# The last scatters, the gates' store, the rows' sum and the last output's scaling in a fused attention and expert kernel: what changes in their order

## The chip, the cores and the metric

The kernel runs on one core of one Trainium2 chip. The metric is the device time of one execution in microseconds (us). TensorE (PE in the profile, its weight loads PEld), VectorE (DVE), ScalarE (ACT), GpSimd (POOL) and SyncE (SP) each run their own instructions in order, and wait for each other by semaphores.

## The reference

Windowed attention over 8 batches, 8 heads, 576 positions and head size 64 gives 4608 rows of 512. Each row then goes to the one expert of eight that its gate logits choose:

```python
x = attn_out.transpose(0, 2, 1, 3).reshape(B * S, H * D)      # 4608 x 512
logits = x @ w_gate                                           # 4608 x 8
expert_idx = argmax(logits, axis=1)
gate_w = softmax(logits)[row, expert_idx]
for e in range(8):
    xe = x[expert_idx == e]
    out[expert_idx == e] = gate_w * (relu(xe @ w1[e]) @ w2[e])   # 512 -> 1024 -> 512
```

All of it is fp32; each large product is made from high and low parts (fp32r).

## The kernel before

**Attention.** The four pairs of batches are cut into nine tiles of 128 rows, 36 steps in all. A step works on several tiles at once, in different stages, and the rows that come out are stored by POOL to `x_d` in DRAM. The first 35 steps stand in a hand-written order; the last ones and the rest up to the experts are ordered by the framework, which keeps the order of the code for each engine except where its model of times puts an instruction earlier. Each row of `x_d` has 512 values of x and 16 copies of the row's gate behind them.

**Routing.** After each pair `route(m)` turns its logits into places: the maximum (`mx`, `sh`), the first expert that has it (`cand`, `fst`, `oh`), counts (`cs`), exponentials and the gate (`ex`, L437 by a helper; `se`, `gate`), which L614 copies sixteen times into `many` and L615 stores by POOL into the last 16 columns of the pair's 1152 rows of `x_d`, 64 bytes a row. Three matmuls with the running counts `crun` give each row's rank in its expert (`rk`, L522 to L526); L530 (`sel`) picks it, and L625 to L632 make from it a position: its block (`blk_i`) and its place in it (`plc_i`).

The positions are written down in two ways. For the first three pairs, each tile of 128 rows is entered by a scatter (L542): an indirect DMA that POOL issues, and that writes row numbers to one of three tables `tab` in DRAM, at the addresses `at_i` that `place` computes. The nine scatters of a pair are put in a list, `slow`, from which every attention step takes one (`pull_spaced`), so the third pair's are issued during the last steps. For the last pair, a table is built in PSUM: `mark` (L557 to L568) makes for each tile a one-hot `s` (by ACT over `off`, or by DVE at L560) and a one-hot `b`, and `enter` (L579) multiplies them into `tb`, in three groups of three. Its steps stand in another list, `side`, in which `off_pe` and `off_both` put work of the other engines and `on_pe` that of TensorE; `pull_pe` and `pull_off` take from it.

**From the tables to the rows.** When all scatters are done, SP reads the three tables into `t_in` (L675) and POOL adds them (L680, L681); DVE makes `scr` from `tb` (L662, L666) and adds the two into `rows_all` (L437 by the helper), which lists the row of every slot of every expert. POOL then gathers rows: `xg<-x_d` (L752), 128 rows and their gates at a time, and these feed the blocks of the experts over transposes by TensorE (`tpx`, L976 and L852).

**Experts.** Meanwhile TensorE works on rows already known, those of expert 0's first tile. Weights come in units of 512 KB (`raw`, L885), which ACT and DVE split into high and low parts (`wu`, L726 and L727). Layer one gives `hps` (L906), from which ACT and DVE make `h` (L917, L918); layer two gives `yps` (L937). After the eight experts and the extra blocks, a loop runs `left` times more, a count that each engine loads from `left` (L1649); in this run it is nought. `finish` (L801) scales `yps` by the gate into `y` on ACT and scatters it to the output by POOL (L802).

Of the kernel before, what the change touches and what calls it, by code (L numbers as in the profile page):

```python
# [11 lines left out]
I32 = mybir.dt.int32  # L12
BF16 = mybir.dt.bfloat16
AF = mybir.ActivationFunctionType
ALU = mybir.AluOpType
# [45 lines left out]
NTHR = 40  # L61
NWARM = 9
GAP, FREE = 3, 35

C_ID, C_TRI, C_REV, C_C0, C_NEW, C_IO, C_ATT = np.cumsum(
    [0, P, P, NE, NE, NE * NT, P]
# [96 lines left out]
def attention_moe_kernel(ctx, tc, qk, v, wg, w, cst, tok, end, slots, mask, zero, out):  # L163
# [30 lines left out]
    sp = att.enter_context(tc.tile_pool(name="sp", bufs=4))  # L194

    late = att.enter_context(tc.tile_pool(name="late", bufs=1))
    t_in = [late.tile([P, NBK], I32, name=f"t_in{i}") for i in range(3)]

    NRQ, NRV = 6, 6
    qkr = fix.tile([P, NRQ, QK], F32, name="qkr")  # L200
# [226 lines left out]
            )  # L427
            lo = end

    side, slow, spare = [], [], []  # L430
    taken = [False]

    def on_pe(f, *a, late=False):
# [28 lines left out]
            side.pop(0)[1]()  # L462

    def pull_spaced():
        if slow:
            slow.pop(0)()

    def pull_off():
# [5 lines left out]
    def route(m, then=None, after=None):  # L474
# [54 lines left out]
        def select():  # L529
            v.tensor_tensor(sel, box["rk"], oh, op=ALU.mult)  # L530
            taken[0] = False

        def place(t):

            t = slice(t, t + 1)
            v.scalar_tensor_tensor(
                at_i[:, t], blk_i[:, t], -(NBK - 1.0 / P), wide[:, t], op0=ALU.mult, op1=ALU.add
            )

        def scatter(t, to, what):  # L540
            place(t)
            nc.gpsimd.indirect_dma_start(  # L542
                out=to[t % 3][:],
                out_offset=bass.IndirectOffsetOnAxis(ap=at_i[:, t : t + 1], axis=0),
                in_=what,
                in_offset=None,
            )
# [25 lines left out]
        def enter(ts):  # L573
# [3 lines left out]
            for t in ts:  # L577
                s1, b1 = hot.pop(t)
                nc.tensor.matmul(box["tb"], lhsT=s1, rhs=b1, start=t == 0, stop=t == NT - 1)  # L579

        on_pe(turn, (0, 1), late=True)
        off_pe(gather_parts, 0)
        off_pe(gather_parts, 1)
# [6 lines left out]
        off_both(  # L590
            lambda: v.scalar_tensor_tensor(cand, sh, 0.0, rev, op0=ALU.is_ge, op1=ALU.mult),
            lambda: v.tensor_reduce(fst, cand, axis=AX.X, op=ALU.max),
        )
        off_both(
            lambda: v.tensor_tensor(
# [8 lines left out]
                op1=ALU.add,  # L604
            ),
        )
        off_pe(nc.scalar.activation, ex, sh, AF.Exp)
        off_both(
            lambda: v.tensor_reduce(se, ex, axis=AX.X, op=ALU.add),
            lambda: v.tensor_scalar_add(se2, se, 1e-9),  # L610
# [1 line left out]
                gate, se2  # L612
            ),
            lambda: v.tensor_copy(many, gate.broadcast_to([P, NT, XP - DM])),  # L614
            lambda: nc.gpsimd.dma_start(  # L615
                x_d[DUMMY + m * S2 : DUMMY + (m + 1) * S2, DM:].rearrange("(t p) o -> p t o", p=P),
                many,
            ),
        )
        if m == NPR - 2:  # L620
            off_pe(hold, True)
# [12 lines left out]
        if m < NPR - 1:  # L634
            off_both(
                lambda: v.tensor_tensor(load, rows_i[:, m], plc_i, op=ALU.subtract),
                lambda: v.tensor_copy(load[:, ::3], rows_i[:, m, ::3]),
                lambda: v.tensor_scalar_mul(wide, posf, float(NBK)),
            )

            def enter_pair():
                v.tensor_tensor(crun, crun, cs[:, :, NT - 1], op=ALU.add)
                for t in range(NT):
                    spaced(scatter, t, tabs, load[:, t : t + 1])
                if then:
                    spaced(then)

            off_pe(enter_pair)
        else:
            off_both(  # L650
                lambda: v.tensor_copy(blk, blk_i),
                lambda: v.tensor_copy(plc, plc_i),
                lambda: v.tensor_tensor(pay, rows_f, plc, op=ALU.subtract),
            )
            off_pe(lambda: v.tensor_tensor(crun, crun, cs[:, :, NT - 1], op=ALU.add))
            for lo in range(0, NT + 3, 3):
                for t in range(lo, min(lo + 3, NT)):
                    off_pe(mark, t)
                if lo:
                    on_pe(enter, range(lo - 3, lo), late=True)  # L660
            off_pe(
                lambda: v.tensor_scalar(  # L662
                    scr, box["tb"], 0.0, float(LAST), op0=ALU.is_gt, op1=ALU.mult
                )
            )
            off_pe(lambda: v.tensor_tensor(scr, box["tb"], scr, op=ALU.add))  # L666
            off_pe(v.tensor_tensor, row_i, t_in[0], scr, op=ALU.add)
        if after:
            after()

# [125 lines left out]
        nc.scalar.copy(x[:, 0], rows)  # L796
        nc.vector.tensor_tensor(x[:, 1], rows, x[:, 0].bitcast(F32), op=ALU.subtract)  # L797

    def finish(y_ps, gate, it_col):
        y = pools["y"].tile([P, DM], F32, name="y")  # L800
        nc.scalar.activation(y, y_ps, AF.Copy, scale=gate)  # L801
        nc.gpsimd.indirect_dma_start(  # L802
            out=out,
            out_offset=bass.IndirectOffsetOnAxis(ap=it_col, axis=0),
# [4 lines left out]
    class Static:  # L809
# [115 lines left out]
                )  # L925
                self.h.append(h)

        def layer2(self, i, fs_=range(8)):
            if fs_[0] == 0:
                self.yps[i] = pools["ps"].tile([P, DM], F32, tag="C", name="yps")  # L930
            yps = self.yps[i]
# [10 lines left out]
                        stop=f == 7 and k == 2,  # L942
                    )
            if fs_[-1] == 7:
                finish(yps, self.gate[i], self.it[i])

    class Dynamic:
        def __init__(self, ti=None, wi=None, fixed=None, units=None, turned=False):
# [300 lines left out]
        step(n)  # L1249
        n += 1  # L1250
    assert not todo and not spare and not turning
    while slow:
        slow.pop(0)()
    while side:
        side.pop(0)[1]()
# [182 lines left out]
    for f in range(4, 8):  # L1438
        st_.layer1([f])
        raw = early.pop(f) if f in early else st_.load(f)  # L1440
        st_.units.append(split_unit(1, raw))
    r0, r1 = rest0
    with tc.manual_schedule(engines=ENGS | {mybir.EngineType.Pool, mybir.EngineType.SP}):
        ahead = nx.ahead
# [100 lines left out]
    with tc.manual_schedule(engines=ENGS | {mybir.EngineType.Pool, mybir.EngineType.SP}):  # L1545
# [97 lines left out]
        dy.layer2()  # L1643
        dz.layer2()
        st_.layer2(2)
        st_.layer2(3)

    left, nbig = info["left"], info["big"]
    extra = nc.values_load(left[0:1, 0:1], min_val=0, max_val=NTHR)  # L1649
    dcur = dsp.tile([P, 1], F32, name="dcur")  # L1650
    nc.vector.memset(dcur, float(DBIG))
    dnum = dsp.tile([P, 1], F32, name="dnum")
# [44 lines left out]
```

## Time and profile before

| | us |
|---|---|
| median of 3 runs | 605.0 |
| the three runs | 604.55, 605.0, 606.33 |
| profiled execution | 608.32 |
| its span | 606.5 |
| PE busy in the span | 587.6 (97%) |
| DVE, ACT, POOL busy | 361.7, 319.0, 185.6 |
| mean granted clock | 0.985 |

A row of the profile gives the line, the engine, the operation and `out<-in` by the names of the program. In rows in order of time the two first numbers are the start and the duration, `x` and a number is how many instructions the row holds, and the bracket is the idle time of the engine ahead of it, with what ended it. In grouped rows the numbers behind the bar are the busy time of all, the mean of one in ns, and idle times. A row with an engine's name and a q is its sequencer.

### The profile page before, as it was taken

What the parts mean: (1) busy time and instruction counts of PE and PEld (TensorE: products, weight loads), DVE (VectorE), ACT (ScalarE), POOL (GpSimd) and SP (SyncE); (2) the same over time, 40 slices, a digit from 0 to 9 for tenths busy, and PEclk for the clock granted to TensorE, in tenths of its full rate; (3) what the DMA queues carried; (4) which work ended last, traced back from release to release, by engine and by line L of the source; (5) the groups of instructions that cost most, each with busy time, mean ns of one, the idle gap of its engine ahead of it and who ended that gap; (6) DMA issues with size and microseconds to landing.
All of it is one profiled execution on the core that took longest, in us unless ns stands there. A gap on an engine that the chain in (4) does not pass through costs nothing. (4 is left out here: it accounts for less than half of the span.)

```text
span 606.5 us, 13511 instructions
## 1 busy us (share of the span) xinstructions
PE 587.6 (97%) x5175; PEld 480.4 (79%) x5175; DVE 361.7 (60%) x780; ACT 319.0 (53%) x624; POOL 185.6 (31%) x234
## 2 busy tenths in 40 slices
PE   7999999999899999999999999999999999999995
PEld 6877777777777888888888888888888887788784
DVE  3876887977668457636564666466555655663200
ACT  2568766666744555534555465455645553562210
POOL 0246577376484225130022012202401220021011
PEclk7899999999899999999999999999999999999998
DMA  8999999995216538986679688788877886789411
GB/s 323 409 367 413 412 407 405 394 340 152 85 52 212 175 124 272 241 289 181 190 261 333 144 266 273 243 222 269 285 232 202 258 294 172 225 267 403 178 44 45
DMA packets 67522, 152.52 MB, mean 251 GB/s; under 512 B 15040, under 2 KB 31360, under 8 KB 67424
## 3 DMA queue, kind: packets, MB, share of 16 engines
q1 hardware_dynamic: 55744, 121.50, 59.4%
q0 software_dynamic: 11712, 30.14, 14.5%
q8 instruction: 41, 0.67, 0.5%
q14 instruction: 25, 0.20, 0.1%
HBM read 124.02 MB, written 28.60 MB: 252 GB/s over the span
## 5 line engine op out<-in xcount | busy, mean ns | idle before, releaser
L727 DVE TENSOR_TENSOR wu<-raw,wu 128x512 fp32r<-128x512 f32 x200 | 128.7, 689 | 61.8 <-ACT wu L726 53.8
L937 PE MATMUL yps<-wu,h 128*128 128x512 f32 x696 | 164.4, 392 | 0.0
L906 PE MATMUL hps<-x,wu 128*128 128x512 f32 (+1 forms) x720 | 161.3, 383 | 0.4 <-DVE h L918 0.4
L906 PEld LDWEIGHTS hps<-x,wu 128*128 128x128 f32 x720 | 132.3, 188 | 27.2 <-DVE h L918 0.8
L937 PEld LDWEIGHTS yps<-wu,h 128*128 128x128 f32 x696 | 129.5, 188 | 27.4 <-issue 0.6
L726 ACT CAST wu<-raw 128x512 fp32r<-128x512 f32 x200 | 112.5, 618 | 11.5 <-DMA raw<-in_w_dram 11.2
L802 POOL DMA_INDIRECT out_dram<-y,rows_all x30 | 30.4, 1014 | 196.1 <-ACT y L801 109.1
L918 DVE SCALAR_TENSOR_TENSOR h<-hps,h 128x512 fp32r<-128x512 f32 (+1 forms) x60 | 40.2, 671 | 52.9 <-ACT h L917 50.2
L323 ACT COPY pts<-pt 96x512 f32<-96x512 f32 x72 | 41.9, 582 | 49.8 <-PE pt L318 40.9
L917 ACT ACTIVATE h<-hps 128x512 fp32r<-128x512 f32 (+1 forms) x60 | 35.0, 583 | 54.5 <-PE hps L906 52.8
L752 POOL DMA_INDIRECT xg<-x_d,rows_all x30 | 30.8, 1027 | 95.9 <-DVE x L797 45.2
L297 DVE TENSOR_REDUCE nm<-s 128x4 f32<-128x384 f32 x72 | 39.6, 551 | 28.1 <-PE s L286 21.3
L318 PE MATMUL pt<-ident,p 128*96 128x128 f32 x288 | 48.2, 292 | 5.2 <-ACT pts L323 4.1
L801 ACT ACTIVATE y<-yps,gate 128x512 f32<-128x512 f32 x30 | 20.6, 688 | 48.9 <-PE yps L937 39.0
L333 PEld LDWEIGHTS o<-vr,pts 96*64 96x64 f32 x1152 | 38.6, 140 | 7.5 <-issue 6.3
L333 PE MATMUL o<-vr,pts 96*64 96x65 f32 x1152 | 44.0, 227 | 0.5 <-issue 0.4
L302 DVE TENSOR_TENSOR d<-s,nm 128x384 f32<-128x384 f32 x72 | 40.0, 557 | 4.6
L1043 PE MATMUL ypd<-wu,hd 128*128 128x512 f32 x168 | 41.0, 392 | 0.2
L312 ACT ACTIVATE p<-d 128x384 f32<-128x384 f32 x72 | 37.6, 524 | 5.7 <-DVE d L302 5.7
L365 POOL DMA_DIRECT2D x_d<-xs x36 | 20.6, 571 | 64.6 <-DVE xs L353 28.4
L318 PEld LDWEIGHTS pt<-ident,p 128*96 128x96 f32 x288 | 29.3, 130 | 13.6 <-ACT pts L323 5.2
L1011 PE MATMUL hpd<-wu,xd 128*128 128x512 f32 x168 | 39.9, 391 | 0.0
(163 smaller groups left out, 626.8 us busy)
## 6 DMA issues: line engine op xcount, KB each, us to landing
raw<-in_w_dram SPq DMA_DIRECT2D x104, 512.0 KB
qkr<-in_qk_dram SPq DMA_DIRECT2D x36, 576.0 KB
vr<-in_v_dram SPq DMA_DIRECT2D x36, 520.0 KB
rows<-xg SPq DMA_DIRECT2D x29, 264.0 KB
xg<-rows SPq DMA_DIRECT2D x116, 64.0 KB
wu<-in_w_dram SPq DMA_DIRECT2D x12, 512.0 KB
x_d<-xs POOLq DMA_DIRECT2D x44, 128.0 KB
wz<-in_w_dram SPq DMA_DIRECT2D x4, 512.0 KB
```

Source lines behind the costliest of these rows:

```text
L297: nc.vector.tensor_reduce(st["nm", n][:, g], st["s", n][g], axis=AX.X, op=ALU.max)
L302: nc.vector.tensor_tensor(st["d", n][:, g], st["s", n][g], st["nm", n][:, g].broadcast_to([P, HP, KB]), op=ALU.subtract,)
L318: nc.tensor.transpose(pt[:KB, h], st["p", n][:, g, h], ident)
L323: nc.scalar.copy(st["pts", n][:, g], st.pop(("pt", n))[:KB])
L333: nc.tensor.matmul(st["o", n][QB * j : QB * (j + 1), g, h], lhsT=pts[:, g, h, QB * j : QB * (j + 1)], rhs=vr[:KB, n % NRV, a : a + DH + 1] ...
L726: nc.scalar.copy(u[:, 0, sl], raw[:, sl])
L727: nc.vector.tensor_tensor(u[:, 1, sl], raw[:, sl], u[:, 0, sl].bitcast(F32), op=ALU.subtract)
L906: nc.tensor.matmul(hps[:, : self.ns], lhsT=u[:, wpart, fs], rhs=self.x[:, xpart, c, : self.ns], start=(k == 0), stop=(k == 11),)
L918: nc.vector.scalar_tensor_tensor(h[:, 1, :n], hps[:, :n], 0.0, h[:, 0, :n].bitcast(F32), op0=ALU.max, op1=ALU.subtract,)
L937: nc.tensor.matmul(yps, lhsT=self.h[f][:, hpart, ts], rhs=u[:, wpart, fs], start=f == 0 and k == 0, stop=f == 7 and k == 2,)
L1011: nc.tensor.matmul(hps, lhsT=self.x[:, xpart, c], rhs=u[:, wpart, ns], start=(k == 0), stop=(k == 11),)
L1043: nc.tensor.matmul(self.yps, lhsT=self.h[f // 4][:, hpart, f % 4], rhs=u[:, wpart, fs], start=f == 0 and k == 0, stop=f == 7 and k == 2,)
```

## The change

The diff, cut to its core (the `t_in` tiles also move: the first one from the pool `late` to the pool `const`):

```diff
+KEPT = 4
...
     def pull_spaced():
-        if slow:
+        if slow and (now[0] < total or len(slow) > KEPT):
             slow.pop(0)()
...
         def select():
             v.tensor_tensor(sel, box["rk"], oh, op=ALU.mult)
             taken[0] = False
-
-        def place(t):
-
-            t = slice(t, t + 1)
-            v.scalar_tensor_tensor(
+            if m == NPR - 1:
+                while slow:
+                    slow.pop(0)()
+                tc.keep_in_program_order(keep_gates())
+
+        def place(lo, hi):
+
+            t = slice(lo, hi)
+            return v.scalar_tensor_tensor(
                 at_i[:, t], blk_i[:, t], -(NBK - 1.0 / P), wide[:, t], op0=ALU.mult, op1=ALU.add
             )

         def scatter(t, to, what):
-            place(t)
+            if now[0] < total or t < NT + 1 - KEPT:
+                place(t, t + 1)
+            elif t == NT + 1 - KEPT:
+                tc.keep_in_program_order(place(t, NT))
             nc.gpsimd.indirect_dma_start(
...
+        def keep_gates():
+            return nc.gpsimd.dma_start(
+                x_d[DUMMY + m * S2 : DUMMY + (m + 1) * S2, DM:].rearrange("(t p) o -> p t o", p=P),
+                many,
+            )
+
...
             lambda: v.tensor_reduce(fst, cand, axis=AX.X, op=ALU.max),
+            lambda: nc.scalar.activation(ex, sh, AF.Exp),
         )
...
-        off_pe(nc.scalar.activation, ex, sh, AF.Exp)
...
-            lambda: nc.gpsimd.dma_start(
-                x_d[DUMMY + m * S2 : DUMMY + (m + 1) * S2, DM:].rearrange("(t p) o -> p t o", p=P),
-                many,
-            ),
+            lambda: None if m == NPR - 1 else keep_gates(),
...
-            off_pe(v.tensor_tensor, row_i, t_in[0], scr, op=ALU.add)
+            finals.append(lambda: v.tensor_tensor(row_i, t_in[0], scr, op=ALU.add))
...
-    def finish(y_ps, gate, it_col):
+    def finish(y_ps, gate, it_col, halved=False):
         y = pools["y"].tile([P, DM], F32, name="y")
-        nc.scalar.activation(y, y_ps, AF.Copy, scale=gate)
+        own = DM // 2 if halved else DM
+        nc.scalar.activation(y[:, :own], y_ps[:, :own], AF.Copy, scale=gate)
+        if halved:
+            nc.vector.tensor_scalar_mul(y[:, own:], y_ps[:, own:], gate)
...
-    while slow:
+    while len(slow) > KEPT:
         slow.pop(0)()
...
         raw = early.pop(f) if f in early else st_.load(f)
         st_.units.append(split_unit(1, raw))
+        if f == 5:
+            tc.keep_in_program_order(finals.pop()())
...
         st_.layer2(2)
-        st_.layer2(3)
-
-    left, nbig = info["left"], info["big"]
-    extra = nc.values_load(left[0:1, 0:1], min_val=0, max_val=NTHR)
+        left, nbig = info["left"], info["big"]
+        extra = nc.values_load(left[0:1, 0:1], min_val=0, max_val=NTHR)
+        st_.layer2(3, halved=True)
+
```

The list `slow` of the third pair ends with the step that reads the tables. `KEPT = 4` keeps that step and the three scatters ahead of it (tiles 6 to 8) from being taken once attention's 36 steps are over; `select` of the last pair takes them, right behind `sel`. `keep_in_program_order` holds an instruction in its place against the framework's reordering.

On POOL, at the end of the routing, before: `tab_64` to `tab_66` are the three tables, `t_in_108` to `t_in_110` their copies.

```order
L542 DMA tab_65<-load,at_i 40960x1
L542 DMA tab_64<-load,at_i 40960x1
L542 DMA tab_66<-load,at_i 40960x1
L615 DMA x_d<-many 128x9x16
L680 TENSOR_TENSOR t_in_108<-t_in_108,t_in_109 128x320
L681 TENSOR_TENSOR t_in_108<-t_in_108,t_in_110 128x320
L752 DMA xg<-x_d,rows_all 128x528 x5
```

And the same place after the change, where the scatter is L550, the store L590, the adds L691 and L692 and the gather L763, with what each waits for in brackets (the semaphores of POOL's DMA queues are DMASW, those of SP's DMAHW):

```order
L550 DMA tab_64<-load,at_i 40960x1 [waits DMASW7_49,DVE_49]
L550 DMA tab_65<-load,at_i 40960x1 [waits DMASW6_49]
L550 DMA tab_66<-load,at_i 40960x1 [waits DMASW0_49]
L691 TENSOR_TENSOR t_in_108<-t_in_108,t_in_109 128x320 [waits DMAHW7_49,DMAHW0_49]
L692 TENSOR_TENSOR t_in_108<-t_in_108,t_in_110 128x320 [waits DMAHW1_49,Pool_49]
L590 DMA x_d<-many 128x9x16 [waits DMASW4_49]
L763 DMA xg<-x_d,rows_all 128x528 [waits DMASW5_49,DMASW4_49,DVE_49]
```

The gates' store has moved from ahead of the two adds to behind them, and the gather waits, as before, for the store's landing (DMASW4) and for `rows_all` on DVE; the first of the three scatters now waits for DVE's merged `at_i`.

On DVE, from the last group's `h` to the next ones, before and after; the `wu` are split weights, `scr` the last pair's rows:

```order
L918 SCALAR_TENSOR_TENSOR h<-hps,h 128x256
L662 TENSOR_SCALAR scr<-tb 128x320
L727 TENSOR_TENSOR wu<-raw,wu 128x512
L666 TENSOR_TENSOR scr<-tb,scr 128x320
L727 TENSOR_TENSOR wu<-raw,wu 128x512
L437 TENSOR_TENSOR rows_all<-t_in_108,scr 128x320
L918 SCALAR_TENSOR_TENSOR h<-hps,h 128x256
L727 TENSOR_TENSOR wu<-raw,wu 128x512 x2
```

```order
L932 SCALAR_TENSOR_TENSOR h<-hps,h 128x256
L673 TENSOR_SCALAR scr<-tb 128x320
L738 TENSOR_TENSOR wu<-raw,wu 128x512
L677 TENSOR_TENSOR scr<-tb,scr 128x320
L738 TENSOR_TENSOR wu<-raw,wu 128x512
L932 SCALAR_TENSOR_TENSOR h<-hps,h 128x256
L738 TENSOR_TENSOR wu<-raw,wu 128x512 x2
L678 TENSOR_TENSOR rows_all<-t_in_108,scr 128x320
```

`rows_all` has moved behind one `h` and two `wu`. Also on DVE, one `at_i` over 128x3 stands between `many` and `posf`, where before the nine single ones had all come earlier.

At the end of the program, after the change, ACT's last rows, DVE's last and POOL's last scatter, each with its waits:

```order
L813 ACTIVATE y<-yps,gate 128x512 [waits DMASW2_49,DMASW4_49,DVE_49,PE_49]
L813 ACTIVATE y<-yps,gate 128x256 [waits DMASW3_49,DMASW5_49,DVE_49,PE_49]
L815 TENSOR_SCALAR y<-yps,gate 128x256 [waits DMASW5_49,Activation_49]
L816 DMA out_dram<-y,rows_all 4736x512 [waits DMASW6_49,DVE_49]
```

Before, the last of these `y` was one ACTIVATE of 128x512 that waited for PE, and the scatter waited for ACT. Now the DVE half waits for ACT's half, and the scatter for DVE. The load of `left` by each engine moved from behind the last `layer2` to ahead of it; SP's moved from the middle of the program to the end with it.

More of the change, by code (lines that the diff above doesn't have):

```diff
@@ L196, in attention_moe_kernel @@
     late = att.enter_context(tc.tile_pool(name="late", bufs=1))
-    t_in = [late.tile([P, NBK], I32, name=f"t_in{i}") for i in range(3)]
+    t_in = [(const, late, late)[i].tile([P, NBK], I32, name=f"t_in{i}") for i in range(3)]
     NRQ, NRV = 6, 6
@@ L428, in st_keep @@
             lo = end
-    side, slow, spare = [], [], []
+    side, slow, spare, finals = [], [], [], []
     taken = [False]
@@ L926, in layer1, with layer2 @@
                 self.h.append(h)
-        def layer2(self, i, fs_=range(8)):
+        def layer2(self, i, fs_=range(8), halved=False):
             if fs_[0] == 0:
@@ L944, in layer2 @@
             if fs_[-1] == 7:
-                finish(yps, self.gate[i], self.it[i])
+                finish(yps, self.gate[i], self.it[i], halved)
     class Dynamic:
```

## The prediction

> **What bounds the kernel now.** I read the page first, then the stretches, then the order of time around the last selection, then the DMA queues there and the end. The page says that TensorE is nearly always busy. The stretches (length, then busy time of PE, PEld, DVE, ACT and POOL) say where it is not.
>
> ```profile
> PE 587.6 (97%) x5175; PEld 480.4 (79%) x5175; DVE 361.7 (60%) x780; ACT 319.0 (53%) x624; POOL 185.6 (31%) x234
> ...
> 170.00:215.00 45.00, 42.88 (x251) 35.76 (x251) 27.88 (x76) 22.67 (x55) 19.97 (x21) 1.00 0.44 141
> 215.00:500.00 285.00, 285.00 (x1280) 236.03 (x1279) 169.21 (x288) 150.98 (x273) 64.03 (x62) 1.00 0.78 243
> 500.00:580.00 80.00, 79.47 (x400) 63.01 (x399) 37.68 (x64) 33.06 (x61) 6.86 (x8) 1.00 0.70 238
> ```
>
> From 215 to 500 us PE has no idle time, from 500 to 580 it has 0.53 us. So time taken out of PE's waits before 215 comes off the end in full, and time put in is never made up. What there is to take is 45.00 - 42.88 = 2.12 us between 170 and 215, where the change works; the one other place that it touches is the end. Now the last selection in order of time (start, duration, idle time and its releaser), with the same step of the previous pair ahead of it:
>
> ```profile
> 166.07 0.39 PE L526 MATMUL rk<-cs,cc 128*128 128x72 f32 x2
> ...
> 166.50 0.23 DVE L530 TENSOR_TENSOR sel<-rk,oh 128x72 f32<-128x72 f32 x1 [0.27 <-PE rk L526]
> ...
> 177.33 0.44 PE L526 MATMUL rk<-cs,cc 128*128 128x72 f32 x2
> 177.48 0.96 POOL L542 DMA_INDIRECT tab<-load,at_i  x1 [0.30 <-issue]
> ...
> 178.54 0.23 DVE L530 TENSOR_TENSOR sel<-rk,oh 128x72 f32<-128x72 f32 x1 [0.84 <-PE rk L526]
> ...
> 178.75 0.97 POOL L542 DMA_INDIRECT tab<-load,at_i  x1 [0.30 <-issue]
> ...
> 179.21 0.17 DVE L630 CAST pos<-posf 128x9 int32<-128x9 f32 x1
> ...
> 180.01 0.69 ACT L557 ACTIVATE off<-ca,plc 128x128 f32<-128x128 f32 x2 [3.04 <-DVE plc L652]
> 180.02 0.97 POOL L542 DMA_INDIRECT tab<-load,at_i  x1 [0.30 <-DVE plc L652]
> ...
> 180.99 1.06 POOL L615 DMA_DIRECT2D x_d<-many  x1
> 181.04 0.41 PE L579 MATMUL tb<-b,s 128*128 128x320 f32 x1 [1.00 <-ACT off L557]
> ...
> 181.32 0.77 DVE L560 TENSOR_SCALAR s<-ca,plc,pay 128x128 fp32r<-128x128 f32 x1
> ...
> 182.15 0.42 PE L579 MATMUL tb<-b,s 128*128 128x320 f32 x1 [0.32 <-DVE s L560]
> ...
> 182.77 0.34 DVE L560 TENSOR_SCALAR s<-ca,plc,pay 128x128 fp32r<-128x128 f32 x1
> ```
>
> In the previous pair `sel` starts 0.04 us after the rank matmuls end (166.46 to 166.50). Here they end at 177.77 and `sel` starts at 178.54, 0.77 later, 0.10 after a scatter on POOL ends (178.44). From `sel` a chain runs over `pos`, `plc` and ACT's `off` to the first `tb` matmul, for which PE idles 1.00 us. The third group waits for DVE's `s`, which took 0.77 us beside the gates' store on POOL (180.99 to 182.05), against 0.34 at 182.77: 0.43 lost, 0.32 of it on PE.
>
> **The three scatters behind the selection.** The scatters at 177.48, 178.75 and 180.02 go behind `sel`. If `sel` was late because POOL was at them, it comes 0.73 sooner (0.77 - 0.04). Ahead of `posf` now stands one `at_i` over 128x3; the nearest row is `pos`, 0.17. The three single ones that go had lain earlier, beside attention, and free nothing. So the chain to `off` gains 0.73 - 0.17 = 0.56 at the first `tb`. With the store away, `s` gains up to 0.32 more on PE: 0.88. From below: the three scatters now run beside the chain, from about 178.5 to 182.2, and if they delay PE's signals as before, half of it is left, 0.4. From above it is both idles whole, 1.00 + 0.32 = 1.3. I take 0.7, nearer to the worked sum than to the ends. Merged `at_i`, exponentials and the first read of the three tables cost nothing beyond this: on DVE and ACT the exponentials keep their place, and SP only reads the tables in another order.
>
> **The gates' store and the rows.** What follows is the second wait that the change touches; the adds, the rows, the gathers and the first use of what they bring:
>
> ```profile
> 184.04 0.39 ACT L917 ACTIVATE h<-hps 128x256 fp32r<-128x256 f32 x1 [0.42 <-DVE s L560]
> ...
> 184.46 0.42 DVE L918 SCALAR_TENSOR_TENSOR h<-hps,h 128x256 fp32r<-128x256 f32 x1 [0.50 <-ACT h L917]
> ...
> 184.82 0.88 POOL L680 TENSOR_TENSOR t_in<-t_in,t_in 128x320 int32<-128x320 int32 x1 [2.77 <-DMA t_in<-tab]
> ...
> 185.78 1.21 POOL L681 TENSOR_TENSOR t_in<-t_in,t_in 128x320 int32<-128x320 int32 x1
> ...
> 187.46 0.48 DVE L437 TENSOR_TENSOR rows_all<-t_in,scr 128x320 int32<-128x320 int32 x1
> ...
> 188.20 1.35 DVE L727 TENSOR_TENSOR wu<-raw,wu 128x512 fp32r<-128x512 f32 x2
> 188.22 1.02 POOL L752 DMA_INDIRECT xg<-x_d,rows_all  x1 [1.23 <-DVE rows_all L437]
> ...
> 189.00 1.47 PE L937 MATMUL yps<-wu,x 128*128 128x512 f32 x5 [0.44 <-DVE wu L727]
> ...
> 195.91 0.59 PEld L976 LDWEIGHTS tpx<-ident,xg 128*128 128x128 f32 x4
> ...
> 200.71 0.60 PE L852 MATMUL tpx<-ident,xg 128*128 128x128 f32 x4
> ```
>
> `rows_all` moves behind an `h` (0.42) and two `wu` (1.35). That lets those pass: PE's 0.44 at 189.00 can go, but only if DVE isn't the next thing late, so I leave it as the upper end and count nothing. By itself `rows_all` then starts about 187.46 + 1.77 - 0.7 = 188.5.
>
> The gathers also wait for the gates' store, since it writes part of the rows that they read. Before, it started at 180.99 and was long done at 188.22. Now it stands behind the adds. The last scatter starts at about 181.1 in place of 180.02, and with it the read of the last table; without the store beside them the reads may run a little quicker, so I put the end of the adds where it was, at 186.99, and let it go as far as 188. Then the store's 1.06 us, and its landing. How long that takes, and a gather's landing, is read from POOL's queue (q0: packets, MB, share of the DMA engines), in the stretch 184 to 185.6 (from 185.6 to 187 there are no packets at all), then 190 to 191 with the weights' queue q1 ahead of it, 191 to 192, and 192 to 193:
>
> ```profile
> q0 software_dynamic: 12, 0.01, 1.7%
> ...
> DMA packets 0, 0.00 MB, mean 0 GB/s; under 512 B 0, under 2 KB 0, under 8 KB 0
> ...
> q1 hardware_dynamic: 157, 0.38, 96.0%
> q0 software_dynamic: 1, 0.00, 1.0%
> ...
> q0 software_dynamic: 64, 0.24, 65.4%
> ...
> q0 software_dynamic: 16, 0.04, 33.8%
> ```
>
> The store's last packets move after 184 and before 185.6, so it lands 3.0 to 4.6 us after its start. The gather of 188.22 has nothing moved by 191 and its 0.28 MB done by 193: 3.8 to 4.8 us, beside weights that fill the DMA engines. Now: store at 187.0, landed at 190.0 to 191.6, first gather then, 2 to 3 us later than before, landed 3.8 to 4.8 after that, 193.8 to 196.4. PE wants it at 195.91 less the gain, 195.2. So the cost lies between 0 and 1.2 us; with the adds as late as 188 it is up to 2.2. I take 0.4, below the middle of 0 to 1.2, since most of the earliest-to-latest stretch lies before the need. The next gather's rows are wanted at 200.71, five microseconds later, and gathers follow each other by 1.3, so they add nothing.
>
> The Trainium skill ("DMA: Bandwidth & Descriptors", section "Anatomy of one DMA — SWDGE (gpsimd) path") gives a DMA issued by GpSimd about 2.0 us plus its bytes at 436 GB/s. By that page the 72 KB store would land after an estimated 2.2 us, at 189.2, and the cost here would be 0; the trace does not agree, with at least 3.0, and the sum keeps the trace's.
>
> **The end.** PE's last matmuls, the last output's scaling, its scatter; then the weight of such an output by form, and of one without a factor from SBUF; then where `left` is loaded, for each engine's sequencer:
>
> ```profile
> 594.74 5.15 PE L937 MATMUL yps<-wu,h 128*128 128x512 f32 x22
> ...
> 599.92 0.69 ACT L801 ACTIVATE y<-yps,gate 128x512 f32<-128x512 f32 x1 [4.75 <-PE yps L937]
> 600.90 0.97 POOL L802 DMA_INDIRECT out_dram<-y,rows_all x1 [2.51 <-ACTq L1653]
> ...
> L801 ACT ACTIVATE y<-yps,gate 128x512 f32<-128x512 f32 x30 | 20.6, 688 | 48.9 <-PE yps L937 39.0 <-issue 7.4 <-ACT wu L726 2.4
> ...
> L1019 ACT ACTIVATE hs<-hpd 128x512 f32<-128x512 f32 x14 | 8.4, 598 | 19.8 <-PE hpd L1011 18.4 <-issue 1.3
> ...
> L1649 PEldq TENSOR_LOAD <-left x1: 545/545/545, 595.7 to 595.7; - x1
> ```
>
> The last `y` becomes ACT on 256 columns and DVE on 256. In the changed order DVE's half waits for ACT's, not for PE, so they run one behind the other. ACT's half costs 0.39 (the `h` of 128x256) plus the 0.09 by which a scaled 512 (0.688) exceeds a plain one (0.598): 0.48. A hand-off is 0.03 (184.43 to 184.46) and DVE's half is like the `h` of 0.42. Sum 0.93 against 0.69: 0.24 slower, and nothing hides it, as POOL's scatter waits for `y`. Side by side it would be 0.69 - 0.48 = 0.21 quicker. I take +0.25, since the wait is in the order.
>
> The Trainium skill ("PSUM — Partial Sum Buffer", section "PSUM bank collisions raise a hardware error") says that no two engines may touch the same PSUM bank and partitions at once, readers too, and that the compiler orders them. It speaks against this halving: by it the sum is +0.24, without it -0.21. No run here shows two engines in one bank at once.
>
> `left` is now loaded ahead of the last 24 matmuls. PE's sequencer ran its load (0.545) at 595.7, over four microseconds ahead of the last matmul's end at 599.89. That lead hides it; were it gone, it would cost 0.55.
>
> **The sum.** -0.7 (selection) + 0.4 (gather) + 0.25 (end) = -0.05, so nothing. The profiled execution took 608.3 us, 606.5 of it span; it would be 608.3 again, and it lies 3.3 over the median of 605.0, which both keep. I forecast 605.0.
>
> **The rivals.**
> *Full gain.* Both idles before `tb` go (1.3), so does the 0.44 at 189.00, the gather lands in time, the end costs 0.25: -1.5, 603.5. For it: that idle is really there, and the gather may land at 193.8. Against it: POOL is still scattering in that stretch. Only if the rest of the 2.12 goes and the halves overlap does it pass -1.8: -2.12 - 0.21 = -2.3, 602.7.
> *The gather behind the gates' store.* Here is the slower side: adds at 188.0, store landed 4.6 later at 192.6, gather landed 4.8 later at 197.4, PE 2.2 late, with a gain of 0.4 and the end's 0.25: +2.05, 607.0. It decides once the first gather lands after 195.2. For it: the weights' queue stands at 96% of the engines from 190 to 191. Against it: it needs every duration at its long end.
> *The selection stays late.* Were `sel` late from PE's own queue, with POOL not the cause, then the change doesn't do what it says: 0 gain, 0.17 for `at_i`, 0.4, 0.25: +0.8, 605.8. Against it: the previous pair, where POOL issued no scatter just then.
>
> **How the numbers follow.** A measurement of this kernel can tell about 0.3% from no change, 1.8 us. The forecast has 0.48 (its own range 604.2 to 605.8), full gain 0.22, the gather 0.2, the late selection 0.1. Faster by over 1.8 us is about half of full gain, 0.1; slower by over it is some half of the gather's, 0.11; the rest, 0.79, is the same. The range goes from 603.4, just past the full gain's own value, to 606.7, which leaves out the worst of the gather's case.
>
> **What would show it.** Right: `sel` starts within 0.1 of the rank's end with the three scatters behind it, the wait before the first `tb` is under 0.6, `s` takes 0.34 at all three places, the gates' store starts near 187, the first gather near 191, PE waits less than 1 us for `tpx`, and the last two halves follow one another, 0.9 together. Wrong: `sel` still 0.7 late, halves that start together, a gather released by `rows_all` alone, or PE waiting over 1.5 us for `tpx`.

## The result: 0.8% slower, and the profile after

| | before | after |
|---|---|---|
| median of 7 runs each, us | 605.37 | 609.71 |
| lowest to highest, us | 604.52 to 608.49 | 608.65 to 613.71 |
| ratio, with its 95% interval | | 1.0080 (1.0058 to 1.0102) |
| profiled execution and its span, us | 608.32, 606.5 | 609.43, 607.6 |

The changed kernel is 4.3 us slower; I had forecast no change and a range up to 606.7. The two profiled executions are only 1.1 us apart, since that of before lay 3 us over its median and that of after near its own. So the spans can't be subtracted; the stretches inside them have to be read. One execution of a later kernel (the kernel before with the later rows' sum) took 2010.82 us and is left out of its ratio. Here are three of those shown before, for the changed kernel (length, then busy time of PE, PEld, DVE, ACT and POOL):

```profile
170.00:215.00 45.00, 41.66 (x239) 34.44 (x232) 27.47 (x76) 21.98 (x54) 19.07 (x20) 1.00 0.47 140
215.00:500.00 285.00, 283.96 (x1274) 234.66 (x1273) 168.94 (x286) 149.99 (x270) 63.83 (x62) 1.00 0.78 243
500.00:580.00 80.00, 80.00 (x405) 64.20 (x404) 38.18 (x64) 34.18 (x63) 7.45 (x7) 1.00 0.70 240
```

PE's idle time from 170 to 215 rose from 2.12 to 3.34 us, where some of it was meant to go, and there is 1.04 us between 215 and 500, where there was none. In order of time, from the end of the rank matmuls (176.04) to the first use of gathered rows:

```profile
175.60 0.44 PE L527 MATMUL rk<-cs,cc 128*128 128x72 f32 x2
...
176.18 0.23 DVE L531 TENSOR_TENSOR sel<-rk,oh 128x72 f32<-128x72 f32 x1 [0.19 <-PE rk L527]
...
176.54 0.15 DVE L541 SCALAR_TENSOR_TENSOR at_i<-blk_i,wide 128x3 int32<-128x3 int32 x1
...
176.96 0.97 POOL L550 DMA_INDIRECT tab<-load,at_i  x1 [1.46 <-DVE crun L666]
...
178.68 0.42 PE L587 MATMUL tb<-b,s 128*128 128x320 f32 x1 [0.23 <-ACT s L566]
...
179.57 1.56 POOL L550 DMA_INDIRECT tab<-load,at_i  x1 [0.30 <-issue]
...
180.08 0.34 DVE L568 TENSOR_SCALAR s<-ca,plc,pay 128x128 fp32r<-128x128 f32 x1
...
185.05 1.20 POOL L692 TENSOR_TENSOR t_in<-t_in,t_in 128x320 int32<-128x320 int32 x1
...
186.20 1.08 POOL L590 DMA_DIRECT2D x_d<-many  x1
186.73 0.48 DVE L678 TENSOR_TENSOR rows_all<-t_in,scr 128x320 int32<-128x320 int32 x1
...
187.23 0.32 SPq L696 DMA_DIRECT2D table<-rows_all  x1
...
187.60 3.03 SPq L899 DMA_DIRECT2D raw<-in_w_dram  x3
...
192.12 1.01 POOL L763 DMA_INDIRECT xg<-x_d,rows_all  x1 [4.84 <-DVE scr L1365]
...
196.08 0.63 PE L990 MATMUL tpx<-ident,xg 128*128 128x128 f32 x4 [2.14 <-DMA xg<-x_d,rows_all]
...
200.67 0.60 PE L866 MATMUL tpx<-ident,xg 128*128 128x128 f32 x4
```

The selection looks as the change wants it: `sel` 0.14 after the rank's end, the wait before `tb` at 0.23, `s` at 0.34. (A second profile of the kernel before, below, shows that it needs no change for that.) Then the gates' store starts at 186.20, and the first gather at 192.12, 4.9 us after `rows_all` is done (187.21). The releaser that the row names, `scr`, had nothing to do with it: the gather waits on DVE for `rows_all`, which was long done, and for the store's landing. The last of the semaphore events of that landing stands in the trace at 191.34, 0.78 us before the gather. PE idles 2.14 us for the gathered rows. At the end the two halves stand one behind the other:

```profile
600.07 0.48 ACT L813 ACTIVATE y<-yps,gate 128x256 f32<-128x256 f32 x1 [4.75 <-PE yps L951]
600.58 0.48 DVE L815 TENSOR_SCALAR y<-yps,gate 128x256 f32<-128x256 f32 x1 [10.10 <-ACTq L1669]
601.34 0.97 POOL L816 DMA_INDIRECT out_dram<-y,rows_all  x1 [3.69 <-DVEq L1669]
```

They take 0.99 us together, 0.30 more than the one of 0.69.

### The profile page after: what moved, and what is told of

Its sections match the earlier page's. It is cut to its first block, busy times and chain, and to the rows that moved or that the text cites. A ratio compares the mean times of both kernels' runs of the same rounds, so it can differ in the third digit from the quotient of the medians.

```text
span 607.6 us, 13506 instructions
## 1 busy us (share of the span) xinstructions
PE 585.6 (96%) x5175; PEld 478.5 (79%) x5175; DVE 362.9 (60%) x779; ACT 319.3 (53%) x624; POOL 186.8 (31%) x234
## 5 line engine op out<-in xcount | busy, mean ns | idle before, releaser
L763 POOL DMA_INDIRECT xg<-x_d,rows_all x30 | 30.6, 1022 | 102.4 <-DMA xg<-rows 75.7
L813 ACT ACTIVATE y<-yps,gate 128x512 f32<-128x512 f32 (+1 forms) x30 | 20.5, 682 | 46.0 <-PE yps L951 30.2
```

## The experiments

The theories: S, the store behind POOL's adds makes the gathers late. K, the three scatters held for the selection are a second cost, as the tables are read later. T, the loss is at the end. D, the changed order of the rows' sum costs. Each ratio below is against runs of the kernel before beside it on the same chip. Each kernel left one profile, too, and since executions differ by 2 us and more, its times are counted from the end of the rank matmuls (their start and duration), in us. `Adds end` is the end of POOL's second add, the next two columns are starts, `PE idle` is PE's idle time just ahead of `yps` (for `wu`) and of the first `tpx` with gathered rows, and `second tpx` is the start of the next four transposes:

| kernel | ratio (95% interval) | adds end | store starts | first gather | PE idle for `wu` | PE idle for `tpx` | second `tpx` |
|---|---|---|---|---|---|---|---|
| before, shown above | 1 | 9.22 | 3.22 | 10.45 | 0.44 | 0 | 22.94 |
| before, second profile | 0.9999 (0.9977 to 1.0021) | 9.51 | 3.33 | 10.31 | 1.17 | 0 | 22.82 |
| changed, shown above | 1.0080 (1.0058 to 1.0102) | 10.21 | 10.16 | 16.08 | 0.69 | 2.14 | 24.63 |
| changed, second profile | 1.0065 (1.0042 to 1.0088) | 10.20 | 10.14 | 15.67 | 0.69 | 2.20 | 24.71 |
| changed, store early | 1.0016 (0.9996 to 1.0037) | 11.28 | 5.01 | 12.09 | 2.06 | 0 | 24.64 |
| the same again | 1.0020 (1.0008 to 1.0033) | 10.99 | 4.98 | 11.80 | 1.49 | 0 | 22.77 |
| changed, end as before | 1.0047 (1.0023 to 1.0071) | 11.01 | 10.95 | 17.56 | 1.44 | 2.89 | 27.34 |
| changed, scatters not held | 1.0036 (1.0018 to 1.0055) | 9.28 | 9.22 | 15.45 | 0.58 | 1.95 | 25.76 |
| changed, store in two | 1.0060 (1.0038 to 1.0081) | 11.26 | 4.99, 11.20 | 13.75 | 1.99 | 2.47 | 27.20 |
| before + late store | 1.0047 (1.0024 to 1.0070) | 9.02 | 8.97 | 15.20 | 1.05 | 1.95 | 24.42 |
| before + held scatters | 1.0037 (1.0015 to 1.0059) | 10.77 | 5.00 | 11.57 | 2.91 | 0 | 25.31 |
| before + later rows' sum | 1.0005 (0.9989 to 1.0021) | 9.44 | 3.35 | 11.27 | 0.29 | 0 | 22.18 |
| the same again | 1.0016 (1.0000 to 1.0033) | 9.61 | 3.38 | 11.44 | 0.53 | 1.10 | 23.63 |
| before + changed end | 1.0004 (0.9987 to 1.0021) | 9.30 | 3.33 | 10.10 | 0.89 | 0 | 22.51 |

The last column holds one thing that none of the theories has. In five of these profiles the granted clock fell to half for 3.41 us, during or just after a long wait of PE: the first with the store early, the end as before, scatters not held, the store in two, and before + held scatters. With the scatters not held, the clock is 0.50 from 193 to 196 us:

```profile
191.78 0.63 PE L990 MATMUL tpx<-ident,xg 128*128 128x128 f32 x4 [1.95 <-DMA xg<-x_d,rows_all]
192.17 2.39 PE L951 MATMUL yps<-wu,h 128*128 128x512 f32 x6
194.36 3.78 PE L1025 MATMUL hpd<-wu,xd 128*128 128x512 f32 x12
```

In the changed kernel's second profile, at the full clock, the same six and twelve matmuls take 1.64 and 2.89 us. So another 1.6 us go, on top of the wait. Between 160 and 590 us the fourteen profiles hold ten waits of 1.95 us or more; five of them have this fall of the clock (the one at 1.95 above, and at 2.06, 2.47, 2.89 and 2.91), five at 1.95 to 2.20 don't, and no shorter wait has it. So a long wait can cost more than itself, and a single profile may show more or less of it than the ratio, which is taken over many executions.

**The changed kernel with the store early.**

```diff
-                while slow:
+                while len(slow) > 1:
                     slow.pop(0)()
                 tc.keep_in_program_order(keep_gates())
+                slow.pop(0)()
```

Expected: 

> The changed kernel with one thing moved: the gates' store stands right behind the three scatters, ahead of POOL's adds. Theory S (the gathers wait for the landing of the store behind the adds): the store starts near 181, some 5 us sooner, the gathers are released by rows_all near 188, PE's wait of 2.14 us ahead of tpx is under 0.3, and 2 to 3 us of the 4.3 lost are back (ratio to before about 1.002 to 1.004). Theory T (the loss sits at the end, in the halved output and the load of left): tpx may come sooner, but the ratio stays at 1.007 or more. Theory D (the selection's order delays the split weights on DVE): the same, 1.007.

Measured 1.0016, 602.98 against 601.51 us. Three quarters of the loss are gone by moving one DMA, as S has it. PE's wait for `tpx` is 0. But K shows as well: PE now idles 2.06 us for split weights (1.49 in the repeat, 1.17 in the second profile of before), behind `rows_all` on DVE, which waits for POOL's adds, which wait for the tables:

```profile
181.05 1.34 POOL L692 TENSOR_TENSOR t_in<-t_in,t_in 128x320 int32<-128x320 int32 x1 [2.92 <-DMA t_in<-tab]
...
183.38 0.49 DVE L679 TENSOR_TENSOR rows_all<-t_in,scr 128x320 int32<-128x320 int32 x1 [1.72 <-POOL t_in L693]
...
184.15 1.02 POOL L764 DMA_INDIRECT xg<-x_d,rows_all  x1 [0.81 <-DVE rows_all L679]
...
184.92 2.12 PE L952 MATMUL yps<-wu,h 128*128 128x512 f32 x5 [2.06 <-DVE wu L739]
```

**The kernel before with the late store alone.**

```diff
             v.tensor_tensor(sel, box["rk"], oh, op=ALU.mult)
             taken[0] = False
+            if m == NPR - 1:
+                tc.keep_in_program_order(keep_gates())
...
-            lambda: nc.gpsimd.dma_start(
...
+            lambda: None if m == NPR - 1 else keep_gates(),
```

Expected: 

> The kernel before with one part of the change: the last pair's gates' store alone goes behind POOL's adds. Theory S: the store starts near 187, lands 5 us later, the first gather starts at 192 to 193 (before 188.2), PE waits 2 us or more for tpx, since here the selection is no earlier; ratio 1.004 to 1.007. Theories T and D: the wait is hidden or small, ratio within 1.002 of before.

Measured 1.0047, 604.55 against 601.51 us. One part of the change, alone, gives over half of the loss, with a wait of 1.95, where S forecast 2 or more.

**The changed kernel with the end as before.**

```diff
-        left, nbig = info["left"], info["big"]
-        extra = nc.values_load(left[0:1, 0:1], min_val=0, max_val=NTHR)
-        st_.layer2(3, halved=True)
+        st_.layer2(3)

+    left, nbig = info["left"], info["big"]
+    extra = nc.values_load(left[0:1, 0:1], min_val=0, max_val=NTHR)
```

Expected: 

> The changed kernel with the end as before: the last output whole on ACT, left loaded behind the last layer. Theory S: the end gives back 0.3 us (0.99 for the two halves against 0.69), ratio about 1.007. Theory T: 1 to 3 us come back, the stretch from PE's last matmul to the end of the span shrinks by 1 us or more, ratio 1.003 to 1.006.

Measured 1.0047: below the 1.007 of S, within the 1.003 to 1.006 of T. But the changed kernel beside the later runs has 1.0065 (1.0042 to 1.0088), and the intervals overlap. Inconclusive by itself; the changed end alone, below, decides it.

**The kernel before, once more.**

Expected: 

> The kernel before, once more, for a second profile and the noise of a ratio: 1.000 within 0.003. If the clock granted in the first profile (0.93 from 150 to 175 us) was an accident of that execution, here rk of the last pair starts 1 to 2 us sooner than at 176.4, and the span is 2 to 3 us shorter than 606.5; every theory expects that.

The ratio is 0.9999. The rank matmuls started 4.3 us sooner than in the first profile and the span is 4.0 shorter, more than the 1 to 2 and 2 to 3 that I had expected. And the profile overturns what I had read from the first one:

```profile
173.00 0.44 PE L526 MATMUL rk<-cs,cc 128*128 128x72 f32 x2
173.26 0.97 POOL L542 DMA_INDIRECT tab<-load,at_i  x1 [0.30 <-issue]
173.48 0.23 DVE L530 TENSOR_TENSOR sel<-rk,oh 128x72 f32<-128x72 f32 x1
...
175.89 0.41 PE L579 MATMUL tb<-b,s 128*128 128x320 f32 x1 [0.15 <-ACT s L558]
...
178.28 0.41 PE L579 MATMUL tb<-b,s 128*128 128x320 f32 x1 [0.34 <-DVE s L560]
...
182.98 0.49 DVE L437 TENSOR_TENSOR rows_all<-t_in,scr 128x320 int32<-128x320 int32 x1 [0.77 <-POOL t_in L681]
...
183.75 1.02 POOL L752 DMA_INDIRECT xg<-x_d,rows_all  x1 [0.80 <-DVE rows_all L437]
...
184.53 1.44 PE L937 MATMUL yps<-wu,x 128*128 128x512 f32 x5 [1.17 <-DVE wu L727]
...
185.11 3.40 SPq L885 DMA_DIRECT2D raw<-in_w_dram  x3
...
191.69 0.49 PE L976 MATMUL tpx<-ident,xg 128*128 128x128 f32 x3
```

`sel` follows the rank's end by 0.04, though a scatter runs on POOL from 173.26 to 174.23. The wait before the first `tb` is 0.15. In all later profiles, of every kernel, `sel` comes 0.03 to 0.04 after the rank. The wait that the held scatters were to remove was one execution's.

**The changed kernel once more.**

Expected: 

> The changed kernel once more, beside the next three and for a second profile. Every theory: ratio to before 1.006 to 1.010, PE waits 1.5 to 3 us for the first tpx, the gates' store starts behind the adds. If the first ratio was high by chance, it comes out at 1.004 to 1.006.

1.0065, 606.07 against 601.48 us: confirmed, with 2.20 before `tpx`.

**The changed kernel with the scatters not held.**

```diff
-KEPT = 4
+KEPT = 0
```

Expected: 

> The changed kernel with the three scatters back where they were (not held for the selection); store, rows' sum and end stay as changed. Theory S (only the store costs): the adds end some 2 us sooner after rk, but the gathers still wait about 6 us for the store, PE waits 2 us for tpx; ratio 1.005, as in the run with the late store alone. Theory K (the held scatters are a second cost, since the tables are read later): 1 to 2 us are back against the changed kernel. From the first rk end to the second tpx: 25 us by S alone, 23.5 to 24.5 by K.

1.0036. The adds end 0.9 sooner, but the store still stands behind them, the gather waits for it, and PE idles 1.95 for `tpx`, as S says; the whole is 0.3% better than the changed kernel, as K says, with intervals that overlap. The second `tpx` came at 25.76, later than both theories had it; 1.6 of that is the half clock shown above.

**The kernel before with the rows' sum later and the exponentials sooner, twice.**

```diff
+            lambda: nc.scalar.activation(ex, sh, AF.Exp),
...
-        off_pe(nc.scalar.activation, ex, sh, AF.Exp)
...
-            off_pe(v.tensor_tensor, row_i, t_in[0], scr, op=ALU.add)
+            finals.append(lambda: v.tensor_tensor(row_i, t_in[0], scr, op=ALU.add))
...
+        if f == 5:
+            tc.keep_in_program_order(finals.pop()())
```

Expected: 

> The kernel before with only two parts of the change: rows_all behind the later h and two wu, exponentials sooner. Theories S and K: rows_all no longer stops DVE for POOL's second add (0.77 in the second profile of before), PE's idle time of 1.17 ahead of yps falls to 0.4 or less, the first gather starts up to 0.7 later without being waited for; ratio 0.998 to 1.000, the only part that gains. Theory D (the rows' move costs, since gathers and table store come later): ratio 1.002 or more.

Expected: 

> The kernel before with rows_all later and exponentials sooner, a second time, to see if this part gains: from rk's end to the second tpx 22.2, against 22.5 to 22.9 with the order of before, ratio 0.998 to 1.000. If the first profile's gain was chance, 22.8 and 1.001.

1.0005, then 1.0016. In the first profile PE's idle time for `wu` fell to 0.29 and the second `tpx` came at 22.18, as hoped. In the second PE waited 1.10 for the gathered rows, and the second `tpx` came at 23.63, later than either case that I had expected:

```profile
183.72 1.55 POOL L762 DMA_INDIRECT xg<-x_d,rows_all  x1 [1.83 <-DVE rows_all L677]
...
183.84 0.42 SPq L898 DMA_DIRECT2D raw<-in_w_dram  x1
...
191.31 0.63 PE L989 MATMUL tpx<-ident,xg 128*128 128x128 f32 x4 [1.10 <-DMA xg<-x_d,rows_all]
```

The gather landed 7.45 us after its start here, 5.85 in the first profile. The later sum does something that I had not seen. With the old order, SP's next load of weights starts 1.5 to 1.6 us after the start of `rows_all`'s table store, in all five profiles that have it, after a `wu` that stands behind `rows_all` (in the second profile of before this ends at 185.08, and the load starts at 185.11). With the later sum those `wu` are done by then, and the load starts 0.37 to 0.38 after the table store, in all nine. Where the gather isn't late, three loads of weights so begin 0.12 to 0.13 us behind it, and with the old order 1.28 to 1.36. What the part gains on DVE, it may lose at the gather; there is no gain to measure, and by the second run rather a small loss. So D isn't excluded, but by these intervals it is at most 0.3%.

**The kernel before with the changed end** (`finish` as in the change).

```diff
-        st_.layer2(3)
-
-    left, nbig = info["left"], info["big"]
-    extra = nc.values_load(left[0:1, 0:1], min_val=0, max_val=NTHR)
+        left, nbig = info["left"], info["big"]
+        extra = nc.values_load(left[0:1, 0:1], min_val=0, max_val=NTHR)
+        st_.layer2(3, halved=True)
```

Expected: 

> The kernel before with only the changed end: the last output in two halves, left loaded sooner. Theories S and K: the halves stand one behind the other, 0.99 against 0.69, the end is 0.3 us later; ratio 1.0005, within noise. Theory T: 1 to 2 us, ratio 1.002 to 1.004, as the difference between the first two ratios (1.008 whole, 1.005 with the end back) would have it; then the stretch from the second tpx to the span's end is longer by that.

1.0004, and the halves take 0.99 against 0.69. T falls: the end costs the 0.3 us that the rows show, and no more that can be measured.

**The kernel before with held scatters** (and the merged `at_i`), the store right behind them.

```diff
+KEPT = 4
...
-        if slow:
+        if slow and (now[0] < total or len(slow) > KEPT):
...
+            if m == NPR - 1:
+                while len(slow) > 1:
+                    slow.pop(0)()
+                tc.keep_in_program_order(keep_gates())
+                slow.pop(0)()
```

Expected: 

> The kernel before with the three scatters held for the selection as in the change, the gates' store right behind them, and nothing else changed (rows_all and the end as before). Theory K (held scatters are a cost of their own): the tables are read later, the adds end 1 to 2 us later after rk, rows_all waits for them and the next h and wu on DVE wait behind it, PE idles 2 us or more ahead of yps; ratio 1.002 to 1.004. Theory S (only the store's place costs): ratio within 1.001.

1.0037. K holds: this part alone costs 2.2 us by the ratio (604.57 against 601.22, 3.4 by the medians). The row of `rows_all`, and of what waits behind it:

```profile
181.31 0.87 POOL L692 TENSOR_TENSOR t_in<-t_in,t_in 128x320 int32<-128x320 int32 x1 [2.88 <-DMA t_in<-tab]
...
183.16 0.49 DVE L438 TENSOR_TENSOR rows_all<-t_in,scr 128x320 int32<-128x320 int32 x1 [2.73 <-POOL t_in L693]
...
184.70 2.50 PE L952 MATMUL yps<-wu,x 128*128 128x512 f32 x5 [2.91 <-DVE wu L739]
```

DVE stands still for 2.73 us. With the later rows' sum, this falls to 1.72 and 0.76 (the changed kernel with the store early, twice). So the two parts seem to belong together: the later sum pays for some of what the held scatters cost, which would be why all parts but the store come to 1.002. The intervals of 1.0037 and 1.0020 overlap, so this rests on the waits, not on the ratios.

**The changed kernel with the store in two.**

```diff
-                tc.keep_in_program_order(keep_gates())
+                tc.keep_in_program_order(keep_gates(1))
                 slow.pop(0)()
+                tc.keep_in_program_order(keep_gates(0, 1))
```

Expected: 

> The changed kernel with the gates' store in two: eight tiles of nine right behind the three scatters, one tile (128 rows of 64 bytes) behind POOL's adds. It tells what the late store's landing is made of. If its size makes it (1152 pieces of 64 bytes): one tile lands 2 to 2.5 us after its start, the first gather starts 3 us after it, PE's wait for tpx is gone, ratio as with the whole store early, 1.002. If the queue of weights makes it: it lands 4 to 5.5 us after, as the whole store did, PE waits 1 to 2 us, ratio 1.005.

Both halves of what I expected came out mixed, and that tells the most. The late tile's 128 rows started at 183.43 and landed at 185.16, after 1.73 us, and the eight early tiles after 2.78, where the whole store had taken 3.67 and 3.89 in that place. So the store's size counts. What the weights add to a whole store this run can't tell, as the late tile was down before the next loads of weights moved anything. The gather started at 185.98, only 1.7 us later than with the whole store early (13.75 against 12.09). But PE still waited 2.47 us, and the ratio was 1.006:

```profile
183.43 0.60 POOL L592 DMA_DIRECT2D x_d<-many  x1
...
184.41 3.03 SPq L901 DMA_DIRECT2D raw<-in_w_dram  x3
...
185.98 1.39 POOL L765 DMA_INDIRECT xg<-x_d,rows_all  x1 [1.95 <-DVE h L934]
...
193.22 0.63 PE L992 MATMUL tpx<-ident,xg 128*128 128x128 f32 x4 [2.47 <-DMA xg<-x_d,rows_all]
```

The gather's landing took 7.1 us here. Its DMA queue (q0, packets, MB, share) and that of the weights (q1), first from 185.98 to 189, then, for the second profile of before, from the gather's start at 183.75 to 188.4:

```profile
q1 hardware_dynamic: 220, 0.82, 87.2%
q0 software_dynamic: 2, 0.01, 4.0%
...
q1 hardware_dynamic: 382, 1.06, 64.5%
q0 software_dynamic: 82, 0.28, 23.2%
```

In the second profile of before, SP issues the next three loads of weights (from 185.11) after the first gather has started, and the gather's 0.28 MB are through in 4.6 us. With the store in two, the weights are issued from 184.41, 1.6 us ahead of the gather, and in its first three microseconds they move 0.82 MB and it 0.01. Being ahead by little need not help, though: the gather of 7.45 above was issued 0.12 ahead of the loads.

**The changed kernel with the store early, again.**

Expected: 

> The changed kernel with the store right behind the three scatters, a second time, since the first profile was of its slowest execution: theory S 1.000 to 1.002, theory K 1.002 to 1.004; from rk's end to the second tpx 22.5 to 23 by S, 24 to 25 by K.

1.0020, and 22.77 to the second `tpx`: S by the stretch, and on the border of both by the ratio.

No version was measurably faster than the kernel before.

## Why the prediction was wrong, by its steps

**The bound** held in the main: PE has hardly any slack from 215 on. It had no term for the half clock that can follow a long wait, nor for waits behind 215.

**The selection, -0.7.** The step that failed first. It took 0.77 us between the rank and `sel` for the kernel's habit, from one execution, and counted 0.56 to 0.88 from it. In twelve other profiles the distance is 0.03 to 0.04, and 0.14 in one. Why it was 0.77 once stays open: that execution had half the clock for 3.41 us, but until 158.28, long before. The comparison with the previous pair should have been with a second execution. The signs that I had named for this step came true (0.14, 0.23, 0.34), but by luck: the second profile of before has 0.04, 0.15 and 0.33 without the change. What the runs leave of the term: the last row of `tb` starts 5.46 to 5.59 after the rank in the changed kernel, and 5.95 in the second profile of before, a gain of 0.4 to 0.5 on PE up to there, the lower end of the range. It does not reach the end: `rows_all` is late by more.

**The held scatters and the adds.** I left the adds' end "where it was" (9.2 us after the rank) and let it go to 188 (10.2). In the runs with the scatters held it came at 10.2 to 11.3, without at 9.0 to 9.6. `rows_all` waits for that, and DVE's splits behind it. The prediction named what is queued behind `rows_all`, but counted nothing for it. The kernel before with this part alone is slower by 0.37%. In the changed kernel PE's idle time for `wu` is no longer than before (0.69), and there the later adds cost by what stands behind them, the store.

**The gather, +0.4.** This step carries most of the miss: the right mechanism, as forecast for the slower rival, in the wrong size. In the prediction's terms, counted from the rank's end, it had the store start at 9.2, land 3.0 to 4.6 later, the gather start at once and land after 3.8 to 4.8, so at 16.0 to 18.6. In the changed kernel's first profile the store started at 10.16 and landed after 5.14 (186.20 to 191.34), the gather started 0.78 after that and landed after 3.83, at 19.9. So three terms were short and the gather's own landing was within its bounds. In all five profiles with the whole store late the landing took 4.7 to 5.8, the gap 0.77 to 0.79, the gather 3.5 to 4.5, and PE waited 1.95 to 2.89, where the term said 0.4 and its range ended at 1.2, or 2.2 with late adds. PE waiting over 1.5 us was the prediction's own sign that it is wrong.

The store's 3.0 to 4.6 was read where it stood early, beside reads in pieces of 1280 bytes. The late one has loads of weights beside it: in the changed kernel one load issued at 184.24, 2 us ahead of it, and three from 187.60 on, 1.4 behind. That they make the landing longer is argued from these places, not shown by itself. The late gather comes 4.5 us behind the first of the three loads, and landed no slower for them.

The prediction gave, beside its own, the Trainium skill's figure ("DMA: Bandwidth & Descriptors", section "Anatomy of one DMA — SWDGE (gpsimd) path"): about 2.0 us plus the bytes at 436 GB/s, an estimated 2.2 for this store. For one tile of it, 8 KB, an estimated 2.0, the trace comes near (1.73 us). For all 1152 rows of 64 bytes it does not agree: 3.4 to 4.5 us where it stood early, 4.7 to 5.8 beside weights. The measurement decides.

**The end, +0.25.** Right: 0.30 by the rows, ACT's half to 600.55, DVE's from 600.58. That agrees with the Trainium skill ("PSUM — Partial Sum Buffer", section "PSUM bank collisions raise a hardware error"), by which two engines are kept out of one bank at a time; no run shows the halves side by side. The load of `left` cost nothing measurable.

**The sum.** Put together from the changed kernel's rows: 1.8 us to the second `tpx` (24.63 against 22.82), 0.3 at the end, 1.0 of new idle time between, 3.1 of the 4.3 by the medians. The other 1.2 are not accounted for; the changed kernel's two profiles kept the full clock there, and how many of the timed executions did is not known. The parts by themselves: late store 1.0047, held scatters 1.0037, later sum 1.0005 and 1.0016, end 1.0004; their sum is over the whole, perhaps since the later sum covers some of the held scatters' cost.

**What stays open.** The 1.0 between 215 and 500. PE's wait stands at 399.81, for DVE's `h`, in the changed kernel, and in its second profile at 354.89, for ACT's `hd`:

```profile
399.81 1.42 PE L920 MATMUL hps<-x,wu 128*128 128x512 f32 x5 [1.04 <-DVE h L932]
...
354.89 1.34 PE L1057 MATMUL ypd<-wu,hd 128*128 128x512 f32 x3 [1.12 <-ACT hd L1046]
```

Two more profiles with the late store have one such (1.10 at 413, 1.25 at 355), a fifth doesn't (0.19), and neither of before has one in that stretch; but with the store early there are some under 0.9. Behind 500 the changed kernel's second profile has one of 1.36 at 509, the store in two one of 1.97 at 510, and the second of before one of 0.82 at 506. Ahead of the waits at 355 and 413, ACT had stood 2.6 to 2.8 us for a load of weights; ahead of that at 399.81, DVE 5.1 us for rows read back. That such loads run late for longer after the stall is my guess; nothing was run to show it. Nor was it tried to hold the weights behind the late gather, which would have shown their share alone.

## What to carry to other kernels

Before a wait is priced, look for it in a second execution: one execution can have a wait that the next doesn't have. When a store moves later in a queue, add up the whole chain, its start, landing, the gap behind it and the next landing, and ask what it now has beside it; here a gather that started 1.7 us later, behind the weights' loads, came over 2 us too late. When an instruction moves ahead of another on an in-order engine, ask which buffers it frees sooner, and what transfer that starts. And a step that waits in the middle of an in-order engine (`rows_all` on DVE) passes every delay of its inputs on to all that is queued behind it.

## What the runs showed of the hardware that was not expected

A DMA of 1152 pieces of 64 bytes (72 KB), issued by GpSimd, landed in 3.4 to 4.5 us beside reads in pieces of 1280 bytes, and in 4.7 to 5.8 where 512 KB loads of weights ran beside it; one of 1024 such pieces in 2.78, one of 128 in 1.73. An instruction that waits for such a landing on POOL started 0.77 to 0.82 us after it.

How long a gather of 128 rows (264 KB) takes to land goes roughly with its distance to the first of three loads of weights on SP's queue. Over thirteen profiles (in the first of before the landing can't be read):

| gather issued | landed after, us |
|---|---|
| 4.1 to 5.6 us behind the first load | 3.5 to 4.5 (five profiles) |
| 1.57 behind | 7.10 (one) |
| 0.12 to 0.13 ahead | 5.20, 5.24, 5.85, 7.45 |
| 1.28 to 1.36 ahead | 3.81, 4.62, 5.64 |

Of ten waits of PE of 1.95 to 2.91 us, five came with 3.41 us at half the granted clock, which cost about 1.6 us more with the scatters not held; none of the shorter waits between 160 and 590 us did.
